# Four chained layers on one core: how the second layer divides by its denominators and projects, with a new planner table

## The chip, the cores and the metric

The kernel runs on one core of one Trainium2 chip. The metric is device time in microseconds (us). Before the change the median of three runs is 1347.23 us (1346.31 to 1350.47). The engines are PE (matrix multiply, writes to the accumulation banks `ps`), ACT (activation functions), DVE (vector work), POOL (a second, slower elementwise engine) and SP, whose queue issues the DMAs.

## The reference

```python
x = A_x                                   # 2048 rows, 512 columns, bfloat16
x = x + A(layernorm(x)); x = x + B(layernorm(x))
x = x + A(layernorm(x)); x = x + B(layernorm(x))

def A(x):   # attention, 32 heads of 16, one k and one v for all heads
    q = x @ wq;  k = x @ wk;  v = x @ wv
    return softmax(q @ k.T / 4) @ v  (heads side by side) @ wo
def B(x):   # linear attention, 32 heads of 16
    q, k, v = x @ wqkv
    pq, pk = phi(q), phi(k)               # phi(t) = (t + 1 if t > 0 else exp(t)) + 1e-6
    kv = sum over rows of pk (outer) v    # per head 16 x 16
    z  = sum over rows of pk              # per head 16
    return (pq @ kv) / (pq @ z + 1e-6) @ wo
```

Layers 0 and 2 are A, layers 1 and 3 are B.

## The kernel before, in words

Rows are handled in 16 tiles of 128. `x_sb` holds all of x, `XT` the transposed normalised tiles, `QT` the transposed queries (in layers 1 and 3 phi of the queries), all in SBUF.

**Layers A.** A layer has 2048 blocks of scores, each 128 keys by 512 (four heads by 128 queries); the two layers together have 4096. PE makes a block (line 1185, "QK"), then its exponential is taken in one of two ways. ACT takes two or three blocks in one instruction (line 1376, `128x1024` or `128x1536`). DVE takes one block with an approximate integer exponential (line 1480, called the fast exponential below), after which POOL makes three shifted copies of it, four blocks at a time (line 1522, `INT64_ADD`). PE multiplies the results with the values and adds them up (line 1239). DVE and POOL may take blocks only once the keys of tiles 0 to 7 exist in that layer; the code's name is `KGATE` = 7, called the gate below. The keys `KM` of tiles 4 to 7 are one group, written by line 1051 (ACT) or 1052 (DVE). On PE, line 1286 is filler without use for the result.

**Layers B.** Each tile gets phi of k, q and v: the exponential on ACT (line 1659), then two steps on DVE (lines 1661 or 776, and 1666). Sums over the rows are gathered in groups of four tiles (`KVG`) and end with the last tile, which is the last tile that layer A gives, so all of a layer B's outputs wait for the end of layer A.

In layer 1 the values lie in `va` with a column of ones behind every 16, so that one product gives kv and z together (line 1923). At the end DVE masks them to block-diagonal form (`kvz`, `zb`, lines 1945, 1949). Then, tile by tile: `den` multiplies `QT` with `zb` (lines 1971, 1973), DVE takes the reciprocal (line 1977); `main` multiplies `QT` with `kvz` (lines 1998, 2029), DVE multiplies with the reciprocals (2002, 2033, into `OB`), the result is transposed (on PE for tiles 0 to 3, by DMA, "va<-va", for tiles 4 to 15, into `OTB`), multiplied with `wo2` and added to x (for tiles 0 and 1 in halves, lines 910, 923, 942; else line 2061).

Layer 3 is built otherwise (`kvt`, `mix`, `den3`, `main3`): kv is multiplied with `wo2` once, giving four matrices M, and a tile's queries are divided by the denominators before one product with M ends the layer.

**Order.** A planner inside the program plays the kernel through with a duration for each operation and writes down the order of each engine's instructions. On the chip every engine runs its list in that order, and an instruction waits where its inputs aren't there. Durations, priorities and the table `TABLE` (from which planned time which set of the planner's numbers holds) so decide how many blocks go to ACT and how many to DVE. The layer-2 tiles follow layer 1 as its outputs come; `MW` and `DW` hold a tile of layer 1 back until a given tile of layer 2 has its normalised rows.

Of the kernel before, what the change touches and what calls it, by code (L numbers as in the profile page):

```python
# [420 lines left out]
class Seg:  # L421
# [46 lines left out]
NOB = 4  # L468
# [29 lines left out]
DENS = {1: [[0], [1], [2], [3], [4], [5], [6], [7], [8, 9], [10, 11], [12, 13], [14, 15]]}  # L498
# [52 lines left out]
MCOP = (DV,)*4  # L551
EVP = 1.2
# [20 lines left out]
    (840, dict(AHEAD=10, BLT=2.2, EVP=1.2, HMAX=0.35, HTOL=0.02, STICK=1.0)),
    (930, dict(AHEAD=10, BLS=1.9, BLT=2.2, EVP=1.2, HMAX=0.35, HTOL=0.02, STICK=1.0)),
    (1110, dict(HMAX=0.1, SPX=1.5, STICK=0.5)),
    (1290, dict(BLS=2.3, BLX=1.0, EVP=0.95, HMAX=0.1, SPX=3.0, STICK=0.5)),
]
BASE = dict(AHEAD=AHEAD, BLS=BLS, BLT=BLT, BLX=BLX, CHT=CHT, DPP=DPP, DXB=DXB, EVP=EVP, FBS=FBS, HMAX=HMAX, HTOL=HTOL, LOW=LOW, OWNP=OWNP, SPX=SPX, STICK=STICK)


def bass_interleave_layers__grouped_kv_mqa__linear_attn_block__prompt_kernel(
# [46 lines left out]
    ones1 = sb("ones1", [1, P], BF16)  # L628
# [1503 lines left out]
```

## Time and profile before

| | |
|---|---|
| runs | 1347.23 us median (1346.31, 1347.23, 1350.47) |
| profiled execution | 1346.96 us, of which 1345.2 us span from first to last instruction, 1.8 us around it |
| granted PE clock | 1.000 |
| ACT busy | 1314.6 us (98%) |
| PE busy | 1301.1 us (97%), with filler |
| DVE busy | 1225.8 us (91%) |
| POOL busy | 1077.2 us (80%) |

A group's row in the profile gives a line, the engine, the shape, a count, the busy time of the group and the mean duration of one. Where instructions overlap at their ends, busy time divided by the count is less than the mean duration: it is what one more of them costs an engine that is full. "Idle before" is the time for which the engine stood still ahead of the group. A timeline row gives start and length in us.

### The profile page before, as it was taken

To read this page: it belongs to the slowest core of one execution; us is meant where nothing else is said; L and a number is where in the kernel's file an instruction comes from. 1 tells how busy PE (TensorE), PEld (TensorE's weight loads), DVE (VectorE), ACT (ScalarE), POOL (GpSimd) and SP (SyncE) were. 2 spreads that over 40 slices of the span, in tenths; PEclk is the share of its full clock that TensorE was granted. 3 is DMA by queue.
4 is the path that set the end of the run, shared out by engine and by line. 5 is a ranking of instruction groups with operands and counts; after the bars stand their busy time and mean duration, and the time that the engine had idled before them with its cause. 6 is when DMAs were issued, how large, how long until landed. Compare 5 with 4: busy or idle time off the path is not lost.

```text
span 1345.2 us, 39031 instructions
## 1 busy us (share of the span) xinstructions
PE 1301.1 (97%) x15334; PEld 436.1 (32%) x15391; DVE 1225.8 (91%) x2224; ACT 1314.6 (98%) x1523; POOL 1077.2 (80%) x1085
## 2 busy tenths in 40 slices
PE   9999999999999999999999999999999999999998
PEld 4322323322232222223643323332232323232335
DVE  8899999899899999997889899989999899999977
ACT  8999999999999999999799999999999999999996
POOL 1699898899989999997005797879989798989870
PEclk9999999999999999999999999999999999999999
DMA  4300000000000000000022000000000000000001
GB/s 107 99 6 13 6 6 13 6 13 2 14 6 13 7 6 6 2 1 2 2 44 45 9 6 13 18 6 6 13 7 9 6 13 6 6 6 1 2 2 64
DMA packets 52517, 20.64 MB, mean 15 GB/s; under 512 B 46192, under 2 KB 51824, under 8 KB 52336
## 3 DMA queue, kind: packets, MB, share of 16 engines
q1 hardware_dynamic: 51280, 18.10, 6.0%
q8 instruction: 125, 2.05, 0.6%
q14 instruction: 56, 0.46, 0.1%
q10 hardware_dynamic: 1056, 0.03, 0.0%
HBM read 5.28 MB, written 2.10 MB: 5 GB/s over the span
## 4 chain that ended last, share of the span: by engine, by line
PE 49%; ACT 30%; issue 9%; DVE 8%; POOL 2%; DMA 1%; ACTq 0%; POOLq 0%; DVEq 0%
ACT W L1376 29%; PE ps L1239 20%; PE ps L1185 16%; PE ps L861 5%; DVE W L1480 4%; PE ps L1064 3%; POOL W L1522 2%; PE ps L904 2%; PE ps L1286 1%; ACT phE L1659 1%; PE ps L1170 1%; DVE sacc L1540 1%; DVE sacc L1666 0%; DVE xn L776 0%; DMA W<-xn 0%
## 5 line engine op out<-in xcount | busy, mean ns | idle before, releaser
L1376 ACT ACTIVATE W<-ps 128x1024 bf16<-128x1024 f32 (+1 forms) x1322 | 1257.4, 1157 | 1.7 <-PE ps L1185 1.5
L1522 POOL INT64_ADD W<-W x1047 | 1070.1, 1036 | 228.2 <-DVE W L1480 174.0
L1480 DVE TENSOR_SCALAR W<-ps 128x512 int16<-128x512 f32 x1394 | 902.8, 682 | 65.9 <-PE ps L1185 54.7
L1239 PE MATMUL ps<-W,VV 128*32 128x512 bf16 x8278 | 631.3, 384 | 3.6 <-DVE sacc L1540 2.4
L1185 PE MATMUL ps<-W,KM 32*128 32x512 bf16 x4096 | 517.6, 385 | 22.2 <-ACT W L1376 12.9
L1185 PEld LDWEIGHTS ps<-W,KM 32*128 32x128 bf16 x4096 | 129.9, 91 | 513.0 <-ACT W L1376 448.0
L1239 PEld LDWEIGHTS ps<-W,VV 128*32 128x32 bf16 x8278 | 149.2, 94 | 250.7 <-issue 176.2
L861 PE MATMUL ps<-wqkv,W 128*128 128x512 bf16 (+1 forms) x226 | 66.8, 368 | 8.0 <-issue 5.1
L1286 PE MATMUL ps<-W,V 128*32 128x512 bf16 (+5 forms) x229 | 61.1, 336 | 1.2 <-DVE W L1666 0.3
L1659 ACT ACTIVATE phE<-ps 128x512 bf16<-128x512 f32 (+1 forms) x66 | 44.4, 675 | 5.2 <-PE ps L1064 4.0
L1540 DVE STREAM_TRANSPOSE sacc<-ps 128x512 f32<-128x512 f32 x52 | 36.8, 707 | 10.1 <-PE ps L1239 10.1
L964 DVE BATCH_NORM_STATS2 st<-x_sb 128x6 f32<-128x512 bf16 x60 | 40.6, 680 | 1.2 <-DMA x_sb<-in_A_x_dram 0.9
L904 PE MATMUL ps<-wo,OT 128*32 128x512 bf16 (+1 forms) x544 | 40.5, 372 | 0.4 <-DVE W L855 0.4
L1064 PE MATMUL ps<-W,wqkv 128*128 128x128 bf16 x512 | 39.5, 220 | 0.4 <-DVE W L855 0.4
L1064 PE MATMUL ps<-W,wq 128*128 128x128 bf16 x464 | 35.6, 220 | 0.6 <-DVE W L1480 0.5
L1064 PEld LDWEIGHTS ps<-W,wqkv 128*128 128x128 bf16 x512 | 29.9, 98 | 10.3 <-issue 7.8
L1064 PEld LDWEIGHTS ps<-W,wq 128*128 128x128 bf16 x464 | 26.1, 98 | 13.7 <-issue 10.4
L776 DVE TENSOR_SCALAR phE<-phE 128x513 bf16<-128x513 bf16 x50 | 21.1, 422 | 10.1 <-ACT phE L1659 8.9
L776 DVE TENSOR_SCALAR xn<-x_sb,mv,rs 128x513 bf16<-128x513 bf16 x52 | 27.0, 532 | 1.8 <-ACT rs L955 1.7
L861 PEld LDWEIGHTS ps<-wqkv,W 128*128 128x128 bf16 x272 | 17.6, 97 | 30.9 <-issue 20.1
L1579 DVE TENSOR_TENSOR Osb<-sacc,ps 128x256 bf16<-128x256 f32 x64 | 26.0, 407 | 0.4
L1286 PEld LDWEIGHTS ps<-W,V 128*32 128x32 bf16 x229 | 18.2, 95 | 24.5 <-issue 10.6
(145 smaller groups left out, 514.3 us busy)
## 6 DMA issues: line engine op xcount, KB each, us to landing
out_dram<-x_sb SPq DMA_DIRECT2D x16, 128.0 KB, 1.7
x_sb<-in_A_x_dram SPq DMA_DIRECT2D x6, 256.0 KB, 5.2
wqkv<-in_B_wqkv_dram SPq DMA_DIRECT2D x1, 1536.0 KB, 8.4
W<-xn SPq DMA_TRANSPOSE x46, 2.5
x_sb<-in_A_x_dram SPq DMA_DIRECT2D x4, 128.0 KB, 2.2
wq<-in_A_wq_dram SPq DMA_DIRECT2D x1, 512.0 KB, 4.3
wo<-in_A_wo_dram SPq DMA_DIRECT2D x4, 128.0 KB, 3.1
wo<-in_B_wo_dram SPq DMA_DIRECT2D x1, 512.0 KB, 9.3
```

Source lines behind the costliest of these rows:

```text
L776: return e.add_instruction(mybir.InstTensorScalarPtr(name=nc.get_next_instruction_name(), engine=mybir.EngineType.DVE, op0=op0, op1=op1, i ...
L861: return e.matmul(dst, lhsT=l, rhs=r, start=(k == 0), stop=(k == len(pairs) - 1))
L904: ins = e.matmul(ps[32 * q:32 * q + 32, b * 512 + cs.start:b * 512 + cs.stop], lhsT=l[:, q, :], rhs=r, start=start, stop=stop)
L1064: ins = e.matmul(dst[:, g * P:(g + 1) * P], lhsT=lhs(g, k), rhs=rhs(k), start=(k == 0), stop=(k == FT - 1))
L1185: return e.matmul(bank(b), lhsT=KM[r, sg.par, kt * P:(kt + 1) * P], rhs=QT[r, sg.t, :], start=True, stop=True)
L1239: ins = e.matmul(ps[32 * j:32 * j + 32, ACC * 512:(ACC + 1) * 512], lhsT=VV[:, kt, 0 if w is None else 1 + w, :], rhs=ap, start=(k == 0), ...
L1286: o = op({PE: (n / 2400.0, lambda e: e.matmul(ps[32 * j:32 * j + 32, b * 512:b * 512 + n], lhsT=V0[:], rhs=QT[:, sg.t, 0:n], start=st, sto ...
L1376: ex = op({AC: (EXO + 0.4267 * n, lambda e, n=n, s_=s_, p_=p_: e.activation(ws_(p_), ps[:, s_ * 512:(s_ + n) * 512], ACTF.Exp, scale=EXPSC ...
L1480: o = op({DV: (0.602, lambda e: e.tensor_scalar(out=dst.bitcast(I16), in0=bank(b), scalar1=VB, scalar2=VLO, op0=ALU.add, op1=ALU.max))}, w ...
L1522: o = op({PO: (512 * m * PSR + PSO, lambda e, g_=g_, f_=f_: e.int64_add(ws_(g_).bitcast(I64), ws_(f_).bitcast(I64), step))}, reads=wk_(f_) ...
L1540: o = op({DV: (TRD, lambda e, src=src: e.transpose(src, bank(ACC)))}, writes=[B_(ACC)] + key, prio=0.0, lat=0.15)
L1659: op({AC: (0.07 + n / 1200.0, lambda e: e.activation(phE[:, i, 0:n], bank(b, n), ACTF.Exp))}, reads=[B_(b)], writes=[("phE", i)], prio=pr ...
```

## The change

In layer 1 the old `kv_`, `den` and `main` go, and the way of layer 3 is used with another way to divide:

- `kvt` now serves layer 1 too: values without the column of ones between heads (the sums z are a product with one column of ones), and M = kv times `wo2` by `mix`, whose four copies from the banks go DVE, ACT, DVE, ACT (`MCO1`). M lies in `va` 0 to 3, kv in `va` 5.
- `denc` makes the denominators of four tiles at once, compact: 16 matmuls with `ZC` (32 columns each) put head h of tile j on row 32j + h of one bank, 128 columns of queries. One Ln and one Exp with scale -1 on ACT (128x128 each) give the reciprocals, in `va` 4.
- `norm1` spreads each reciprocal over the head's 16 rows and multiplies `QT` with it: for tiles 0 to 3 by four matmuls with a constant `E4` (made on POOL at the start) and a DVE multiply from the bank; for tiles 4 to 15 by four DMAs on SP's queue from 8 rows to 128 rows, 256 bytes each, into one of three buffers, and a DVE multiply of two SBUF operands. After the gate of layer 2 that multiply runs over a rearranged order of elements (`turn`).
- `main3` multiplies the divided queries with M and adds x (tiles 0 and 1 in halves).
- Gone per tile: the reciprocal on DVE, the product with `kvz`, the DVE multiply of its 512 columns from a bank, the transpose and its copy.
- The value product of layers 0 and 2 (`a_v`) has 16 columns instead of 128.
- The late tiles' queries of layer 1 have a pool of their own (`NB1`), and `TABLE` is another one.

```diff
@@ a_v
-            mm(v[:, i, :], [(XT[:, t, ft, :], wkv[:, ft, 0:P]) for ft in range(FT)], [XK_(t), "wv", "wkr"], b, prio, 0.25)
+            mm(v[:, i, 0:DH], [(XT[:, t, ft, :], wv[:, ft, :]) for ft in range(FT)], [XK_(t), "wv"], b, prio, VDUR)
@@ table
-    (840, dict(AHEAD=10, BLT=2.2, EVP=1.2, HMAX=0.35, HTOL=0.02, STICK=1.0)),
...
+    (840, dict(AHEAD=10, BLS=1.9, BLT=2.9, BLX=1.0, DXB=0.3, HMAX=0.2, HTOL=0.06, LOW=6, OWNP=4.0, SPX=4.0)),
...
@@ kvt, at the end, L == 1
+                    o = op({DV: (0.13, lambda e, b=bs[1]: e.tensor_tensor(
+                        out=ZC[:].rearrange("p (g c) -> p g c", c=40)[:, :, 0:8], in0=bank(b, 4).unsqueeze(2).to_broadcast([P, 4, 8]),
+                        in1=mask8[:, :, 0:1].rearrange("p h o -> p (h o)").unsqueeze(1).to_broadcast([P, 4, 8]), op=ALU.mult))},
+                           reads=["mask8"], writes=[B_(bs[1]), "ZC"], prio=pr - 0.05)
+                    pl.process(denc(0, DENC[0], bs[1]))
@@ mix
-            c = op({MCOP[g]: by[MCOP[g]]} if MCOP else by, writes=[B_(b), ("W", g), ("M", g)], prio=pr)
+            c = op({MCOP[g]: by[MCOP[g]]} if L == 3 else {MCO1[g]: by[MCO1[g]]}, writes=[B_(b), MK(g), ("M", g)], prio=pr, over=under(g))
@@ new: denc and norm1
+            def fn(e):
+                for g in range(4):
+                    for j, t in enumerate(ts):
+                        ins = e.matmul(ps[32 * j:32 * j + 32, b * 512:b * 512 + P], lhsT=ZC[:, 32 * g:32 * g + 32], rhs=QT[:, t, g * P:(g + 1) * P],
+                                       start=(g == 0), stop=(g == 3))
+            op({PE: (0.3, fn)}, reads=[QK_(t) for t in ts] + ["ZC"], writes=[B_(b)], prio=pr, lat=0.2, mode="col").cols = 512
+            op({AC: (DC1[0], lambda e: e.activation(bank(b, P), bank(b, P), ACTF.Ln, bias=epsc[:]))}, reads=["epsc"], writes=[B_(b)], prio=pr if pl.calm else 0.9)
+            o = op({AC: (DC1[1], lambda e: e.activation(vm_(4)[:, P * gi:P * gi + P], bank(b, P), ACTF.Exp, scale=-1.0))}, writes=[B_(b), ("rec", gi)],
+                   prio=pr - 0.01 if pl.calm else 0.9, over=[("va", 4)])
...
+            if t not in PEX:
+                i = yield ("acq", rb_pool, pr)
+                rb = vm_(i)
+                for g in range(4):
+                    op({SP: (0.07, lambda e, g=g: e.dma_start(rb[:, g * P:(g + 1) * P], vm_(4)[32 * j + 8 * g:32 * j + 8 * g + 8, P * gi:P * gi + P].unsqueeze(1).to_broadcast([8, DH, P])))},
+                       reads=[("rec", gi)], writes=[("rb", i, g)], prio=pr, lat=DBL, dma=True, over=[("va", i), "kvT"] if i == 5 else [("va", i)])
+                yield from until(*[("rb", i, g) for g in range(4)])
+                if ("K", 2, KGATE) in pl.flags:
+                    o = op({DV: (0.6, lambda e: e.tensor_tensor(out=turn(q), in0=turn(q), in1=turn(rb), op=ALU.mult))},
...
+                else:
+                    o = op({DV: (0.34, lambda e: e.tensor_tensor(out=q, in0=q, in1=rb, op=ALU.mult))},
...
+            op({PE: (0.23, fn)}, reads=[("rec", gi), ("E4", j)], writes=[B_(b)], prio=pr, lat=0.2).cols = 512
+            o = op({DV: (0.6, lambda e: e.tensor_tensor(out=q, in0=q, in1=bank(b), op=ALU.mult))}, writes=[B_(b), QK_(t), ("qn", t)], prio=pr)
@@ main3, now for layer 1 too
+            if t in MCRIT[L]:
+                bs = yield from acq2(pr)
+                proj2(bs, lambda g: qn[:, g * P:(g + 1) * P], lambda g, hs: at(g)[:, hs], t, keys, pr)
...
-        def kv_(gi, ts):
-        def den(ts):
-        def main(t):
...
```

Line numbers move by up to 13 before layer B's code: the exponentials are lines 1376 and 1480 before and 1387 and 1491 now, QK is 1185 and 1196, layer 1's addition to x is 2061 and 1986. Counted over the whole order of the engines, these counts differ:

| engine, operation | before | now |
|---|---|---|
| ACT exponential, two blocks (`128x1024`) | 1264 | 1259 |
| ACT exponential, three blocks (`128x1536`) | 58 | 58 |
| ACT exponential, one block (`128x512`) | 0 | 1 |
| DVE fast exponential, one block | 1394 | 1403 |
| of these in layer 0 / layer 2 | 718 / 676 | 715 / 688 |
| ACT Ln and Exp of `denc` (`128x128`) | 0 | 8 |
| ACT copy of M (`128x512`) | 0 | 2 |
| ACT copy of `OTB` (`128x512`, `128x256`) | 1, 2 | 0, 0 |
| ACT `KM` (`128x512`, `128x256`) | 3, 2 | 2, 0 |
| DVE `KM` (`128x512`, `128x256`) | 9, 2 | 10, 4 |
| SP transposes of `va` / spreading DMAs | 12 / 0 | 0 / 48 |

**ACT between layer 1's last sums and layer 2's first normalisation.** Before (phE is phi's exponential, x_sb the addition to x, va the copy of a transposed tile, ve and rs the normalisation):

```order
L1696 CAST va<-ps 128x16x16 x2
L1659 ACTIVATE phE<-ps 128x512 x2
L877 COPY va<-ps 128x256
L942 CAST x_sb<-ps 128x256
L877 COPY va<-ps 128x256
L942 CAST x_sb<-ps 128x256
L953 ACTIVATE ve<-mv,eps 128x1
L955 ACTIVATE rs<-ve 128x1
```

Now:

```order
L1707 CAST va<-ps 128x256 x2
L1672 ACTIVATE phE<-ps 128x512
L1911 ACTIVATE ps<-ps,epsc 128x128
L1912 ACTIVATE va<-ps 128x128
L1852 CAST va<-ps 128x512
L1672 ACTIVATE phE<-ps 128x512
L1852 CAST va<-ps 128x512
L1672 ACTIVATE phE<-ps 128x512
L953 CAST x_sb<-ps 128x256 x2
L964 ACTIVATE ve<-mv,eps 128x1
L966 ACTIVATE rs<-ve 128x1
```

Ln and Exp (1911, 1912) and two of the four copies of M (1852) stand now between the last sums and the addition to x; the copies of transposed tiles are gone.

**DVE in the same place.** Before (zb and kvz are the masks, rdB the reciprocals, L2002 the multiply with them, L936 the statistics of x):

```order
L1945 TENSOR_TENSOR zb<-ps,mask 128x8
L1945 TENSOR_TENSOR zb<-ps,mask 128x24
L1949 TENSOR_TENSOR kvz<-ps,mask 128x128
L1949 TENSOR_TENSOR kvz<-ps,mask 128x384
L1977 RECIPROCAL rdB<-ps 128x32 x2
L1661 TENSOR_SCALAR phE<-phE 128x512
L2002 TENSOR_TENSOR va<-ps,rdB 128x256 x4
L876 COPY va<-ps 128x256
L1666 SCALAR_TENSOR_TENSOR W<-ps,phE 128x512
L1661 TENSOR_SCALAR phE<-phE 128x512
L936 BN_STATS st<-ps 128x6 x2
```

Now (ZC and the mask of kv, the copies of M, the multiply of the queries in `W`):

```order
L1817 TENSOR_TENSOR ZC<-ps,mask 128x4x8
L1829 TENSOR_TENSOR va<-ps,mask 128x512
L1674 TENSOR_SCALAR phE<-phE 128x512
L1852 CAST va<-ps 128x512
L1959 TENSOR_TENSOR W<-W,ps 128x512
L1852 CAST va<-ps 128x512
L1959 TENSOR_TENSOR W<-W,ps 128x512
L1679 SCALAR_TENSOR_TENSOR W<-ps,phE 128x512
L947 BN_STATS st<-ps 128x6 x2
```

Two copies of M and two multiplies stand now where the reciprocals, four half multiplies and a copy stood.

**PE where the keys of tiles 4 to 7 are made in layer 2.** W,wkv with 512 columns is their product (four matmuls), W,KM is QK, wkv,W the value product, W,VV the product with the values. Before:

```order
L1185 MATMUL ps<-W,KM 128x512 x3
L861 MATMUL ps<-wkv,W 128x128 x3
L861 MATMUL ps<-W,wkv 128x512
L1185 MATMUL ps<-W,KM 128x512 x2
L861 MATMUL ps<-W,wkv 128x512 x3
L861 MATMUL ps<-wkv,W 128x128 x4
```

Now:

```order
L872 MATMUL ps<-wkv,W 128x16 x8
L1250 MATMUL ps<-W,VV 32x512 x4
L1196 MATMUL ps<-W,KM 128x512 x3
L872 MATMUL ps<-W,wkv 128x512 x3
L1196 MATMUL ps<-W,KM 128x512 x2
L872 MATMUL ps<-W,wkv 128x512
```

The rows look alike, but the place is another: counted from layer 2's first QK, the last matmul of these keys stands behind 84 blocks of QK before and behind 64 now.

More of the change, by code (lines that the diff above doesn't have):

```diff
@@ L467 @@
 RING = 24
-NOB = 4
 DTL = 3.6
@@ L551 @@
 MCOP = (DV,)*4
+MCO1 = (DV, AC, DV, AC)
+DC1 = (0.31, 0.26)
+SPL = False
+DCP = 1.3
+NB1 = 3
+VDUR = 0.16
+PEX = range(4)
+DBL = 2.6
 EVP = 1.2
@@ L1872, in main3 @@
         def main3(t):
             pr = 1.5 + 0.02 * t
-            yield ("flag", ("qn", t))
+            yield ("flag", ("qn", L, t))
             for g in range(4):
-                yield ("flag", ("M", g))
+                yield ("flag", ("M", L, g))
             yield from until(("qn", t), *[("M", g) for g in range(4)])
+            if L == 1 and MW[t] is not None:
+                yield ("flag", ("xnT", 2, MW[t]))
+                yield from until(XK_(MW[t]))
+            qn = QT[:, t, :] if L == 1 else W[:, 4 + t, :]
@@ L2067, in main @@
+            if L == 1 and t in QHOLD[2]:
                 lend_after(("x", L, t), NW + t)
@@ L2071, in run_b @@
             pl.process(q_(t))
-            pl.process((main3 if L == 3 else main)(t))
-        for ts in DENS.get(L, ()):
-            pl.process(den(ts))
+            pl.process(main3(t))
         if L == 3:
```

328 lines of the change are left out of this document (110 added, 218 removed).

## The prediction

> **What bounds the kernel now.** I read the page's first part, then the busy time of every engine by stretches.
>
> ```profile
> span 1345.2 us, 39031 instructions
> PE 1301.1 (97%) x15334; PEld 436.1 (32%) x15391; DVE 1225.8 (91%) x2224; ACT 1314.6 (98%) x1523; POOL 1077.2 (80%) x1085
> ```
>
> ```profile
> core 0: us, PE busy (x) PEld busy (x) DVE busy (x) ACT busy (x) POOL busy (x), PEclk, DMA share, GB/s
> 0.00:50.00 50.00, 45.66 (x439) 21.96 (x440) 41.50 (x107) 43.62 (x59) 11.91 (x43) 1.00 0.53 136
> 50.00:600.00 550.00, 538.20 (x6432) 160.20 (x6449) 516.46 (x894) 549.76 (x617) 515.58 (x507) 1.00 0.04 8
> 600.00:660.00 60.00, 57.92 (x771) 31.00 (x769) 48.94 (x114) 50.10 (x78) 29.59 (x31) 1.00 0.01 2
> 660.00:700.00 40.00, 38.09 (x378) 17.83 (x382) 29.98 (x62) 39.52 (x49) 0.00 (x0) 1.00 0.20 36
> 700.00:1300.00 600.00, 580.43 (x6903) 182.25 (x6927) 557.54 (x981) 599.29 (x682) 512.26 (x500) 1.00 0.05 10
> 1300.00:1345.20 45.20, 40.84 (x427) 22.85 (x431) 31.39 (x69) 32.29 (x43) 7.81 (x8) 1.00 0.14 48
> ```
>
> PE and ACT both look full, but PE's time holds filler, and ACT is the one without gaps: from 50 to 600 us it stands still for 0.24 us, from 700 to 1300 for 0.71. Its 30.6 us of idle time (1345.2 - 1314.6) lie at the start (6.4 in the first 50 us), at the passage from layer 0 through layer 1 to layer 2 (9.9 between 600 and 660) and at the end (12.9). So the time is ACT's work plus the idle time of these three places, and a change counts by what it does to either. DVE and POOL matter because each block that DVE takes is one that ACT needn't, and these blocks begin only at the gate. POOL's 0.00 between 660 and 700 shows where layer 2 runs without that help.
>
> What an exponential costs ACT, and the other ACT rows that the change touches:
>
> ```profile
> L1376 ACT ACTIVATE W<-ps 128x1024 bf16<-128x1024 f32 x1264 | 1183.9, 1140 | 1.4 <-PE ps L1185 1.3
> L1376 ACT ACTIVATE W<-ps 128x1536 bf16<-128x1536 f32 x58 | 85.5, 1521 | 0.3 <-PE ps L1185 0.2
> L1051 ACT ACTIVATE KM<-ps,kmask 128x512 bf16<-128x512 f32 x3 | 2.1, 712 | 1.4 <-DVE KM L1052 1.4
> L1051 ACT ACTIVATE KM<-ps,kmask 128x128 bf16<-128x128 f32 x5 | 1.8, 364 | 0.6 <-PE ps L861 0.5
> L1727 ACT CAST va<-ps 128x512 bf16<-128x512 f32 x2 | 1.4, 704 | 0.0
> L1051 ACT ACTIVATE KM<-ps,kmask 128x256 bf16<-128x256 f32 x2 | 0.9, 473 | 0.3 <-PE ps L861 0.2
> L877 ACT COPY va<-ps 128x256 bf16<-128x256 bf16 x2 | 0.7, 373 | 0.0
> L855 ACT COPY va<-ps 128x512 bf16<-128x512 bf16 x1 | 0.6, 580 | 0.0
> ```
>
> Two blocks cost 1183.9 / 1264 = 0.937 us, three 85.5 / 58 = 1.474, so a third block costs 0.54 and one alone about 0.5 (0.937 less a block of the first kind, half of it).
>
> **The change part by part.** *ACT's exponentials.* By the counts, five instructions of two blocks go and one of one block comes: -5 x 0.937 + 0.5 = **-4.2 us**. The nine blocks go to DVE. Where from: layer 2 gives DVE 12 more, layer 0 three fewer. The layer-2 gain is the earlier gate: the keys of tiles 4 to 7 stand behind 64 QK blocks instead of 84, and 20 blocks at half of 0.937 are 9.4 us of ACT. In the trace the gate is here:
>
> ```profile
> 700.20 0.75 DVE L1052 TENSOR_SCALAR KM<-ps,kmask 128x512 bf16<-128x512 f32 x1 [1.75 <-PE ps L861]
> 700.86 0.68 DVE L1480 TENSOR_SCALAR W<-ps 128x512 int16<-128x512 f32 x1
> ```
>
> *ACT's other work.* The eight Ln and Exp of 128x128 are in no row; the same shape as `KM` takes 0.364, so 8 x 0.36 = +2.9 (bounds 1.5, half of it, where their ends overlap, to 3.8, with the 0.473 of the row of 256 columns). Two copies of M at 0.704: +1.4. Three copies of transposed tiles: -0.58 - 2 x 0.37 = -1.3. `KM` on ACT: -0.71 - 2 x 0.47 = -1.65. Together **+1.35**. [...]
>
> *A wait that goes.* At 44 us ACT stood still behind DVE for the second half of a group of layer 0's keys; in the new order ACT writes both halves of one itself there:
>
> ```profile
> 44.15 0.69 ACT L1051 ACTIVATE KM<-ps,kmask 128x512 bf16<-128x512 f32 x1 [1.35 <-DVE KM L1052]
> ```
>
> That is **-1.35** of ACT's idle time. What is late next there is PE's matmul for these keys, which both halves wait for in either order; if it comes late too, half of it returns.
>
> *The passage.* The chain from the last sums to layer 2's first exponential, and the gaps in it:
>
> ```profile
> 644.17 0.41 PE L1923 MATMUL ps<-va,sacc 128*128 128x136 bf16 x4
> 644.64 0.25 DVE L1945 TENSOR_TENSOR zb<-ps,mask 128x8 bf16<-128x8 f32 x2
> 645.50 0.56 DVE L1977 RECIPROCAL rdB<-ps 128x32 f32<-128x32 f32 x2
> 646.24 1.42 DVE L2002 TENSOR_TENSOR va<-ps,rdB 128x256 bf16<-128x256 f32 x4
> 647.93 0.78 PEld L923 LDWEIGHTS ps<-wo,va 128*128 128x128 bf16 x8
> 648.60 0.87 DVE L936 BATCH_NORM_STATS2 st<-ps 128x6 f32<-128x256 f32 x2
> 655.84 1.06 PE L1089 MATMUL ps<-W,wq 128*128 128x128 bf16 x16
> 657.36 0.39 PE L1185 MATMUL ps<-W,KM 32*128 32x512 bf16 x2
> 657.79 1.02 ACT L1376 ACTIVATE W<-ps 128x1024 bf16<-128x1024 f32 x1 [0.48 <-PE ps L1185]
> ```
>
> Before, the sums end at 644.58 and the projection of tile 0 starts 3.4 us later. Now there are two strands. Denominators: mask 0.25, 16 matmuls about 0.5, Ln 0.36, Exp 0.36, four spreading matmuls 0.4, with about 0.3 for the handing over, ready for the multiply at 2.3. M: mask of kv, matmul, four copies, two of them on DVE. DVE must do mask 0.6, copy 0.6, multiply 0.6, copy 0.6 in that order, with waits for the first matmul and for the spreading: the fourth ends at about 3.6. So tile 0 comes some 0.2 us later than before; tile 1, whose multiply follows at once, some 0.4 earlier than its transposes and copies let it. Behind that, the first QK stood behind the 16 matmuls of tile 1's queries (655.84, 1.06 us); in the new order it stands ahead of them, waiting only for tile 1's keys. DVE's order has two more long steps (0.6 each) before tile 0's statistics, which takes most of that back. I take **-0.5**, with bounds of -1.5 (all of the 1.06 and tile 1's 0.4) and +1.5 (two DVE steps of 0.6 with waits). ACT's additional work in the passage is counted above.
>
> *The spreading DMAs.* A transposing issue holds SP for 1.19 us, a plain one less:
>
> ```profile
> L2086 SPq DMA_DIRECT2D out_dram<-x_sb x16: 332/332/368, 1327.2 to 1342.9; - x16
> out_dram<-x_sb SPq DMA_DIRECT2D x16, 128.0 KB, 1.7
> L869 SPq DMA_TRANSPOSE va<-va x12: 1188/1190/2096, 672.9 to 731.8; - x12
> va<-va SPq DMA_TRANSPOSE x12, 2.8
> ```
>
> At 0.33 us an issue and 1.7 to landing, four DMAs of a tile land 3 x 0.33 + 1.7 = 2.7 us after they may start, about what one transpose took. Three buffers let the first three tiles go at once: the third lands after 11 x 0.33 + 1.7 = 5.3 us, and the planner reckons 0.07 an issue and 2.6 to landing, 3.4 in all. DVE's list has the third multiply right behind the first two, so it waits up to 2 us there, and behind it are queued phi's steps, whose banks PE wants. DVE has 10.0 of 40 us free between 660 and 700, and ACT then has tile 0's and 1's blocks to go on with: I take **+0.5**, bounds 0 to +2. The 48 issues take 16 us of SP in place of 12 x 1.19 = 14.3; the transposes of layer 2's rows queue behind them, which is in the same half us.
>
> *What counts nothing.* PE loses work in both the value product and layer 1; ACT doesn't wait for it in the long stretches (1.3 us before 1264 exponentials, first row above), so it becomes filler. The constants on POOL come before its first blocks, in 38 us of the first 50 that are free; if they came late, only tiles 0 to 3 of layer 1 would ask for them, 600 us later.
>
> Sum against the profiled execution: 1346.96 - 4.2 + 1.35 - 1.35 - 0.5 + 0.5 = **1342.8 us**. That execution lies 0.27 below the median of the runs, so against the median of 1347.23 the forecast is 0.33% faster. What a measurement of this kernel can tell from no change is about 0.3%, 4 us: below 1343.2 counts as faster, above 1351.3 as slower. The forecast lies only 0.4 inside.
>
> **The rivals.** *1. DVE and POOL collide, no change to speak of.* The multiply of the spread reciprocals has two SBUF operands. Before, such a multiply ran only at the end, with POOL still:
>
> ```profile
> L1867 DVE TENSOR_TENSOR W<-W 128x512 bf16<-128x512 bf16 x16 | 6.1, 418 | 0.0
> L1522 POOL INT64_ADD W<-W x1047 | 1070.1, 1036 | 228.2 <-DVE W L1480 174.0
> ```
>
> In the new order four or five of them come behind the gate, with POOL at work. If the two engines exclude each other, each may wait one POOL addition: 4 x 1.04 = 4.1 us on a DVE that is 93% full from there on (557.54 of 600), passed on through PE to ACT: 1346.9, the same as before. [...] No run here shows it, and four tiles have little weight; I give it 0.15.
>
> *2. The gain is eaten by small waits, no change.* The work saved on ACT is only 2.85 us; if the passage goes to its upper bound and the DMAs too, the sum is 1346.96 - 4.2 + 1.35 - 1.35 + 1.5 + 2 = 1346.3. For it speaks that two unlike orders meet the chip's durations with other slack; against it that ACT stood still for under 1 us in 1150 us of the long stretches. This, and smaller misses of the kind that leave the time between 1343.2 and 1346, have 0.22.
>
> *3. The DMAs are slow, slower than before.* If a spreading DMA holds SP as a transpose does, 1.19 us, and lands after 2.8, the third tile lands after 11 x 1.19 + 2.8 = 15.9 us instead of 5.3. DVE, PE and ACT run in order, so most of the 10.6 comes through, less what DVE's slack takes: about 10 us, 1352.8. It turns slower from 8.5 us on, that is from about 1.05 us an issue. A plain issue of 0.33 speaks against it; the broadcast of one row to 16 and the 256 bytes are in no row. 0.11.
>
> *4. The change does less than the order says:* the keys of tiles 4 to 7 are late on the chip and DVE's additional blocks hold up PE. That is rival 2 with the place at the gate; it has no chance of its own.
>
> **How the numbers follow.** The forecast has 0.52, rivals 1 and 2 (no change) 0.37, rival 3 (slower) 0.11. The lower end takes the passage's and the activations' lower bounds: 1342.8 - 1.0 - 1.4 - 0.5 (no DMA wait) = 1339.9, and 1.5 more, since ACT's start and end may gain as the passage did: 1338.5. The upper end holds rivals 1 and 2 with half of a DMA term on top: 1346.9 + 1 = 1348. Rival 3 and a faster end beyond 1338.5 are left out, under 2 in 10.
>
> **What would show it.** Right: ACT's busy time near 1311.8 us; 1403 fast exponentials, the first of layer 2 some 8 us earlier in the span than 700.86; no gap ahead of `KM` at 44 us; ACT's idle time from 600 to 660 near 9.4; the four DMAs of a tile landing within 3 us. Wrong: ACT idle for more than 2 us between 660 and 1300 (rivals 2 and 3, told apart by whom DVE's multiply of the queries waits for), a multiply of 1 us or more beside POOL (rival 1), or an issue of a spreading DMA near 1 us.

## The result and the profile after

The changed kernel takes **1359.72 us** (median of 4 runs, 1357.32 to 1361.96) against 1348.49 for the kernel before (1346.31 to 1350.47; four runs, the three of the table above among them). The ratio is 1.0083, interval 1.0062 to 1.0105: slower by 0.83%. The forecast was 1342.8, faster. The profiled execution took 1360.89 us.

The page of the changed kernel, span and engines:

```profile
span 1359.1 us, 39265 instructions
PE 1321.0 (97%) x15441; PEld 434.8 (32%) x15441; DVE 1237.8 (91%) x2219; ACT 1315.0 (97%) x1523; POOL 1089.3 (80%) x1094
```

Busy time by stretches of the changed kernel, cut as in the prediction (last columns: granted TensorE clock, DMA share, GB/s):

```profile
0.00:50.00 50.00, 45.79 (x430) 20.47 (x430) 39.78 (x105) 42.95 (x59) 12.65 (x45) 0.93 0.53 138
50.00:600.00 550.00, 542.09 (x6478) 161.90 (x6476) 513.63 (x887) 549.92 (x616) 511.49 (x502) 1.00 0.04 7
600.00:660.00 60.00, 59.80 (x797) 30.13 (x794) 49.79 (x105) 51.58 (x80) 33.05 (x33) 1.00 0.01 2
660.00:700.00 40.00, 36.29 (x361) 16.92 (x360) 32.25 (x73) 34.82 (x51) 0.00 (x0) 0.96 0.30 43
700.00:1300.00 600.00, 581.70 (x6781) 178.28 (x6780) 557.62 (x962) 589.16 (x662) 512.71 (x498) 0.98 0.05 9
1300.00:1359.10 59.10, 55.37 (x604) 27.08 (x604) 44.69 (x93) 46.52 (x60) 19.44 (x19) 1.00 0.11 37
```

ACT's work hardly changed (1315.0 against 1314.6). Its idle time rose from 30.6 to 44.1 us, and the rows say where: 5.18 us between 660 and 700 where it was 0.48 (+4.7), and 10.84 between 700 and 1300 where it was 0.71 (+10.1); the start loses 0.7, the passage and the end win 1.8. The clock column has numbers below 1.00 in the rows of 660 and 700, and at the start. A finer cut of the same view, first the kernel before, then the changed one:

```profile
660.00:680.00 20.00, 18.80 (x196) 9.20 (x197) 14.36 (x30) 19.60 (x24) 0.00 (x0) 1.00 0.09 15
700.00:720.00 20.00, 18.93 (x183) 6.28 (x184) 19.43 (x37) 19.74 (x25) 9.34 (x9) 1.00 0.13 27
720.00:740.00 20.00, 18.20 (x166) 5.83 (x168) 18.59 (x34) 19.84 (x27) 10.55 (x11) 1.00 0.26 52
740.00:760.00 20.00, 19.12 (x218) 6.42 (x216) 16.90 (x31) 19.97 (x25) 14.31 (x14) 1.00 0.07 15
```

```profile
660.00:680.00 20.00, 16.60 (x178) 8.99 (x177) 14.26 (x32) 14.94 (x22) 0.00 (x0) 0.91 0.32 41
700.00:720.00 20.00, 15.76 (x101) 3.83 (x103) 19.21 (x28) 14.79 (x17) 6.72 (x5) 0.78 0.27 42
720.00:740.00 20.00, 18.23 (x166) 5.14 (x158) 18.42 (x31) 16.71 (x19) 12.06 (x11) 0.84 0.12 21
740.00:760.00 20.00, 19.99 (x195) 5.37 (x195) 17.67 (x31) 18.03 (x22) 15.06 (x15) 0.87 0.07 15
```

So nearly the whole loss lies in two places: ACT works 4.7 us less between 660 and 680 and 10.0 less between 700 and 760. The timeline of the second, in DVE's, PE's, POOL's and ACT's rows (start, length, and in brackets the idle time ahead with what ended it):

```profile
704.47 2.45 DVE L1941 TENSOR_TENSOR W<-W,va 128x512 bf16<-128x512 bf16 x1
...
706.98 0.39 PE L872 MATMUL ps<-va,W 128*128 128x512 bf16 x1 [1.41 <-DVE W L1941]
...
707.54 4.87 POOL L1533 INT64_ADD W<-W  x3 [71.32 <-DVE W L1491]
...
707.96 2.91 DVE L1941 TENSOR_TENSOR W<-W,va 128x512 bf16<-128x512 bf16 x1
...
711.45 0.61 PE L1196 MATMUL ps<-W,KM 32*128 32x512 bf16 x3 [2.24 <-DVE W L1491]
...
712.10 1.02 ACT L1387 ACTIVATE W<-ps 128x1024 bf16<-128x1024 f32 x1 [2.42 <-PE ps L1196]
```

`L1941` is the multiplication of the queries behind the gate, the one whose operands go through `turn`: its view `p (g c) -> p c g` with 128 columns in `c` makes neighbouring elements lie 128 columns apart. It takes 2.45 us, and did so the first time with POOL still idle; the same multiplication ahead of the gate (`L1944`, no `turn`) takes 0.42. Four of them hold DVE for 8 us more than the plan's 0.6 each, PE stands still behind them, and then PE itself is slow: three QK matmuls take 0.61 us at 711.45, at a granted clock of 0.50, where they took 0.39 at 703.35, at 1.00.

The first place, 660 to 680, in the same view, with the rows for the spreading DMAs' line (duration min/median/max) and DVE's wait for them (total, times, longest) ahead:

```profile
L1937 SPq DMA_DIRECT2D va<-va x48: 607/607/807, 658.4 to 709.3; - x48
```

```profile
DVE W L1944 <- DMA va<-va: 4.2, 2, 2.2
```

```profile
665.61 0.42 DVE L1944 TENSOR_TENSOR W<-W,va 128x512 bf16<-128x512 bf16 x1 [2.25 <-DMA va<-va]
...
666.43 1.70 PE L872 MATMUL ps<-va,W 128*128 128x512 bf16 x4 [2.16 <-DVE W L887]
668.35 0.42 DVE L1944 TENSOR_TENSOR W<-W,va 128x512 bf16<-128x512 bf16 x1 [1.98 <-DMA va<-va]
...
669.01 0.60 ACT L1672 ACTIVATE phE<-ps 128x512 bf16<-128x512 f32 x1 [3.31 <-PE ps L1075]
```

An issue holds SP for 0.607 us, not 0.33. The second and third multiplication wait for their DMAs; PE, in order, stands still for 2.16 us, runs four matmuls in 1.70 us behind that, and ACT waits 3.31. The clock fell here too: 0.91 on the average of these 20 us.

### The profile page after: what moved, and what is told of

Read it like the earlier page. It is cut to its first block, busy times and chain, and to the rows that moved or that the text cites. A ratio compares the mean times of both kernels' runs of the same rounds, so it can differ in the third digit from the quotient of the medians.

```text
span 1359.1 us, 39265 instructions
## 1 busy us (share of the span) xinstructions
PE 1321.0 (97%) x15441; PEld 434.8 (32%) x15441; DVE 1237.8 (91%) x2219; ACT 1315.0 (97%) x1523; POOL 1089.3 (80%) x1094
## 4 chain that ended last, share of the span: by engine, by line
PE 52%; ACT 29%; issue 8%; DVE 8%; POOL 3%; DMA 1%; SPq 0%; ACTq 0%; DVEq 0%; POOLq 0%
ACT W L1387 27%; PE ps L1250 22%; PE ps L1196 17%; PE ps L872 4%; PE ps L1075 3%; POOL W L1533 3%; DVE W L1491 2%; PE ps L1297 2%; PE ps L915 2%; ACT phE L1672 1%; DVE st L975 1%; DVE xn L781 0%; DVE W L1941 0%; SPq L1937 0%; DVE KM L1063 0%
## 5 line engine op out<-in xcount | busy, mean ns | idle before, releaser
L1491 DVE TENSOR_SCALAR W<-ps 128x512 int16<-128x512 f32 x1403 | 912.0, 682 | 71.1 <-PE ps L1196 58.1
L1250 PE MATMUL ps<-W,VV 128*32 128x512 bf16 x8305 | 638.5, 386 | 4.6 <-DVE sacc L1551 3.1
L1250 PEld LDWEIGHTS ps<-W,VV 128*32 128x32 bf16 x8305 | 152.0, 94 | 260.4 <-issue 169.8
L872 PE MATMUL ps<-wqkv,W 128*128 128x512 bf16 (+1 forms) x272 | 76.5, 371 | 0.4 <-DVE sacc L1679 0.3
L1297 PE MATMUL ps<-W,V 128*32 128x512 bf16 (+6 forms) x243 | 67.8, 352 | 1.7 <-DVE W L866 0.8
L1075 PEld LDWEIGHTS ps<-W,wq 128*128 128x128 bf16 x464 | 26.2, 98 | 13.5 <-issue 9.5
```

The source lines that it names most:

```text
L872: return e.matmul(dst, lhsT=l, rhs=r, start=(k == 0), stop=(k == len(pairs) - 1))
L1075: ins = e.matmul(dst[:, g * P:(g + 1) * P], lhsT=lhs(g, k), rhs=rhs(k), start=(k == 0), stop=(k == FT - 1))
L1250: ins = e.matmul(ps[32 * j:32 * j + 32, ACC * 512:(ACC + 1) * 512], lhsT=VV[:, kt, 0 if w is None else 1 + w, :], rhs=ap, start=(k == 0), ...
L1297: o = op({PE: (n / 2400.0, lambda e: e.matmul(ps[32 * j:32 * j + 32, b * 512:b * 512 + n], lhsT=V0[:], rhs=QT[:, sg.t, 0:n], start=st, sto ...
L1491: o = op({DV: (0.602, lambda e: e.tensor_scalar(out=dst.bitcast(I16), in0=bank(b), scalar1=VB, scalar2=VLO, op0=ALU.add, op1=ALU.max))}, w ...
```

## The experiments

Three theories stood after the result: **A**, the turned order of elements makes the multiplication slow by itself (rival **B**: it collides with POOL); **C**, the DMAs' issues, one behind another, set the wait at 660 (rival **D**: the landing does); and **E**, the new order or its table is to blame for all of it.

**1. Plain multiplications.**

```
-    e.tensor_tensor(out=turn(q), in0=turn(q), in1=turn(rb), op=ALU.mult)
+    e.tensor_tensor(out=q, in0=q, in1=rb, op=ALU.mult)
```

> Edit: the four multiplications of the queries behind the gate read and write their columns in plain order instead of the turned one (stride of 128 columns inside); every instruction stands where it stood in the changed kernel. Theory A (shape): the turned multiplication takes 2.43 us by itself, whatever POOL does; it holds DVE, PE stands still behind it and its granted clock halves. Then the plain ones take 0.42 us with POOL at work, the clock stays at 1.00 between 700 and 760 us, ACT's busy time there returns from 49.5 to about 59.5 us, and the time is 1359.7 - 10 = about 1349.5 us. Rival B (collision): the multiplication is long because POOL is at work. Then the plain ones take 1 to 1.5 us (0.42 and up to one POOL addition of 1.04), the clock still falls once or twice, and the time is 1354 to 1359 us.

Measured: 1349.05 us (10 runs, 1345.8 to 1351.39), ratio to before 1.0001 (0.9988 to 1.0015). By stretches, and the rows of the four multiplications, with those of POOL's additions during which two of them ran:

```profile
660.00:680.00 20.00, 16.53 (x165) 7.99 (x162) 13.85 (x32) 15.36 (x22) 0.00 (x0) 0.91 0.27 35
700.00:720.00 20.00, 18.94 (x178) 5.67 (x176) 20.00 (x40) 20.00 (x24) 9.39 (x9) 1.00 0.32 50
720.00:740.00 20.00, 19.81 (x215) 5.97 (x215) 19.50 (x37) 20.00 (x24) 16.31 (x16) 1.00 0.11 21
740.00:760.00 20.00, 19.35 (x219) 6.09 (x215) 18.53 (x31) 20.00 (x22) 17.92 (x18) 1.00 0.01 2
```

```profile
702.25 0.42 DVE L1941 TENSOR_TENSOR W<-W,va 128x512 bf16<-128x512 bf16 x1
703.87 0.90 DVE L1941 TENSOR_TENSOR W<-W,va 128x512 bf16<-128x512 bf16 x1
707.98 0.40 DVE L1941 TENSOR_TENSOR W<-W,va 128x512 bf16<-128x512 bf16 x1
722.18 0.39 DVE L1941 TENSOR_TENSOR W<-W,va 128x512 bf16<-128x512 bf16 x1
...
703.45 3.35 POOL L1533 INT64_ADD W<-W  x3 [69.78 <-PE ps L1297]
...
721.22 3.38 POOL L1533 INT64_ADD W<-W  x3 [2.93 <-PE ps L1250]
```

A is shown, with every row in its old place. ACT works 60.00 of the 60 us from 700 to 760 (49.53 in the changed kernel) at the full clock. Of the two multiplications that ran beside POOL's additions, one took 0.90, 0.5 longer, and one 0.39. The trace of experiment 7, with the same order, has 0.90 at the same place and 0.42 and 0.40 for its other two plain ones. So a lengthening like the one B speaks of is seen at that one place, and costs DVE 0.5 us in the whole kernel. In the changed kernel POOL loses more than DVE: a group of three additions beside a turned multiplication takes 4.87 us (row of 707.54) where it takes 3.35 here. The loss between 660 and 680 is untouched.

**2. The planner is told the price of an issue** (turned multiplications kept, order planned anew).

```
-    op({SP: (0.07, lambda e, g=g: e.dma_start(rb[...], ...))}, ..., lat=DBL, ...)   # DBL = 2.6
+    op({SP: (0.61, lambda e, g=g: e.dma_start(rb[...], ...))}, ..., lat=DBL, ...)   # DBL = 2.4
```

> Edit: the planner is told that a spreading DMA holds SP for 0.61 us and lands 2.4 us after that, in place of 0.07 and 2.6; the order is planned anew, the turned multiplications stay. Theory C (issue): the loss between 660 and 680 us comes from the issues, one behind another on SP, for which the plan had left no time. Then DVE's wait for the DMAs (4.2 us) goes to under 0.5, ACT's busy time from 660 to 680 rises from 14.9 to 19 or more, and the time is about 1359.7 - 4.7 = 1355 us, with the loss behind 700 us still there. Rival D (the landing, or the passage itself): the wait stays above 2 us or is replaced by another on PE before 680 us, and the time stays at 1358 or above.

Measured: 1359.22 us, ratio 1.0079 (1.0055 to 1.0103).

```profile
660.00:680.00 20.00, 19.47 (x216) 10.32 (x215) 18.14 (x42) 19.34 (x30) 0.00 (x0) 1.00 0.35 47
...
700.00:720.00 20.00, 15.48 (x125) 4.36 (x122) 19.07 (x29) 14.15 (x17) 7.03 (x8) 0.84 0.17 26
720.00:740.00 20.00, 19.86 (x144) 4.30 (x142) 15.45 (x27) 15.37 (x17) 9.12 (x10) 0.66 0.08 15
```

DVE's wait for the DMAs is gone, and ACT works 19.34 of the 20 us from 660 on at the full clock, as C said. The time did not follow: the new order has 1394 fast exponentials in place of 1403, so the exponentials cost ACT 1271.5 us in place of 1266.5. In all ACT has 3.1 us more work (1318.1 against 1315.0), which takes back the 3.3 us of idle time that went (40.8 against 44.1). The four turned multiplications (2.54 us on the average) cost what they did before: ACT works 49.51 of the 60 us from 700 on. The wait is settled, C's time was missed by 4 us.

**3. and 4. Spreading by matmuls**, for all tiles, and for tiles 4 to 7 beside plain multiplications:

```
-PEX = range(4)
+PEX = range(16)        # 3: all tiles
+PEX = range(8)         # 4: with plain multiplications
```

> Edit: the reciprocals of all 16 tiles are spread by matmuls into PSUM, as those of tiles 0 to 3 are already; there are no spreading DMAs and no turned multiplication. Theories A and C together: both losses go, 10 us behind 700 and 4.7 between 660 and 680, while twelve multiplications read PSUM at 0.64 us in place of 0.42 (+2.6 us on DVE, not on ACT): about 1359.7 - 14.7 = 1345 us, at most 1348. Rival E (the new order or its table is to blame): the granted clock falls again in the same places, and the time stays above 1352 us.

Measured: 1348.93 us (10 runs), ratio 1.0009 (0.9993 to 1.0025). ACT is busy for 19.28 us from 660 to 680 and for all 60 from 700 to 760, at a clock of 1.00. Both losses are gone with the new table still in place, so the table isn't their cause; the order was planned anew, and for the order it is experiment 1 that speaks. That it isn't below 1348, as expected, has two reasons: the replanned order leaves ACT 1317.5 us of work in place of the 1312.5 with plain multiplications, and 5 of the 10 runs have a mean clock of 0.998 or less (median of the others 1347.5).

> Edit: plain multiplications, and the reciprocals of tiles 4 to 7 are spread by matmuls too, so that DMAs spread only tiles 8 to 15, which are wanted later. Theories A and C: no wait of DVE for DMAs over 0.5 us, the granted clock at 1.00 from 660 to 760 us, and the time 1344 to 1347 us. If the multiplications of tiles 8 to 15 collide with POOL (B), they take 1 us or more each, and the time is 1348 or above. Rival E as for the kernel without DMAs: above 1352 us.

Measured: 1357.81 us, ratio 1.0071 (1.0046 to 1.0096). A miss: this order leaves ACT 1320.6 us, DVE waits for DMAs for 4.9 us at other places ahead of the gate (3.21 of them at 680.30), and the start lost 2 us against before at a clock of 0.87. A small edit changes everything behind it in the plan; so of the experiments below all but the last keep the rows of PE, DVE and ACT where they were, apart from two DMA issues on ACT in experiment 6.

**5. Two queues for the early DMAs.**

```
-    op({SP: (0.07, lambda e, g=g: e.dma_start(rb[...], ...))}, ...)
+    op({PO if t < 8 and g > 1 else SP: (0.07, lambda e, g=g: e.dma_start(rb[...], ...))}, ...)
```

> Edit: plain multiplications, and of the four spreading DMAs of each of tiles 4 to 7 two go out on POOL's queue, where POOL stands still until the gate; PE, DVE and ACT keep the order of the changed kernel row for row. Theory C (the issues, one behind another on SP, set the wait): DVE's 4.4 us of waiting for the DMAs go to under 1, ACT's busy time from 660 to 680 rises from 15.4 to 19 or more, and the time falls by 3.5 to 4.5 us against the kernel with plain multiplications (1349.05 as median, 1345.8 in its runs at the full granted clock): to about 1342 at the full clock, 1345 as a median. Rival D (the landing sets it, or POOL's queue is as slow): the wait stays above 2.5 us and the time does not move by 2.

Measured: **1344.53 us** (12 runs, 1342.34 to 1348.84), ratio to before **0.9974** (0.9962 to 0.9986): faster than both kernels. The line's rows, DVE's wait, and the stretch:

```profile
L1939 SPq DMA_DIRECT2D va<-va x40: 607/607/850, 655.8 to 705.8; - x40
L1939 POOL DMA_DIRECT2D va<-va x8: 590/621/787, 656.1 to 661.6; - x8
...
DMA to landing us min/median/max: 2.5/2.8/4.5
```

```profile
DVE W L1946 <- DMA va<-va: 2.2, 1, 2.2
```

```profile
660.00:680.00 20.00, 17.36 (x176) 8.62 (x176) 15.12 (x34) 16.48 (x24) 1.18 (x2) 0.91 0.21 29
```

Half of the wait went, from 4.4 to 2.2, and the median fell by 4.5 us against plain multiplications. Only 2.2 of these lie in the runs at the full clock (1343.6 against 1345.8, table of experiments 8 to 10); the rest comes with fewer runs at a low clock, 5 of 12 in place of 7 of 10. C expected a wait under 1 us and holds for half of it; the other half is left to the landing (D) or to the issues that remain. Two of each early tile's four issues, at 0.607 us each, are gone from SP's row of issues.

**6. Three queues.**

```
+    op({AC if t < 6 and g == 3 else PO if t < 8 and g in (1, 2) else SP: (0.07, ...)}, ...)
```

> Edit: plain multiplications, and the spreading DMAs of the early tiles go out on three queues (tiles 4 and 5: one on SP, two on POOL, one on ACT; tiles 6 and 7: two on SP, two on POOL), PE, DVE and ACT otherwise in unchanged order. Theory C (the number of issues ahead of a tile's last DMA sets the wait): the wait of 2.2 us for tile 5 that is left with two queues falls under 1.2, the two issues on ACT cost it at most 1 us in a gap, and the time is 0.5 to 1.5 us under that of the kernel with POOL's queue alone (1342.3 to 1344.3 in its runs at the full clock). Rival D (the DMA engines, which work at 0.2 to 0.35 of their time, or the landing set it): the wait stays at 2 us or more, and the time is the same or, by the issues on ACT, up to 1 us longer.

Measured: 1346.09 us (12 runs, 1343.21 to 1349.43), ratio 0.9981 (0.9969 to 0.9994). The wait was 1.4 in place of 2.2, not under 1.2 as C expected, and ACT works 18.49 us from 660 to 680 in place of 16.48, at a clock of 1.00 in place of 0.91; from 600 to 660 it loses 0.6. In the runs at the full clock the time is 1343.3 against 1343.6, but 8 of 12 runs, not 5, had a lower clock, the profiled one among them, which lost 1.0 us between 20 and 40 at a clock of 0.91. The third queue's gain is thus at most 0.3 us, and the median is not below that of two queues. Nor is the shorter wait shown to be its work: the kernel of experiment 9, with two queues, waits 1.5 us in its trace (0.40 and 1.09), at a clock of 1.00 and with 18.29 us of ACT.

**7. One turned multiplication**, tile 15's, the other three plain.

> Edit: of the four multiplications behind the gate only that of tile 15 is turned; the other three are plain, every instruction stands where it stood. It tells the stall from what follows it. Theory K (the clock): the turned multiplication takes 2.43 us in place of 0.4; PE stands still behind it for over 1 us, and its granted clock then lies at 0.50 for 8 to 10 us, in which PE does 4 to 5 us less; ACT loses 3 to 4.5 us in all, most of them after the multiplication has ended: 1348.8 to 1350.3 at an otherwise full clock, against 1345.8. Rival L (the stall alone): ACT loses at most the 2.0 us by which the multiplication is longer, all of it within 3 us of its end, and the clock stays at 1.00: 1347.8 at most.

Measured: 1352.02 us (12 runs, 1348.27 to 1356.99), 3.0 above the kernel with four plain ones. It starts at 725.34 and takes 2.45 us; by stretches of 2 us:

```profile
726.00:728.00 2.00, 0.19 (x3) 0.11 (x2) 2.00 (x2) 1.53 (x2) 2.00 (x1) 1.00 0.33 66
728.00:730.00 2.00, 1.94 (x13) 0.51 (x12) 1.86 (x4) 0.97 (x2) 1.42 (x3) 0.80 0.00 0
730.00:732.00 2.00, 2.00 (x17) 0.57 (x13) 1.86 (x4) 1.99 (x3) 1.90 (x2) 0.50 0.00 0
732.00:734.00 2.00, 2.00 (x18) 0.47 (x20) 1.27 (x4) 1.04 (x3) 1.04 (x1) 0.50 0.00 0
734.00:736.00 2.00, 2.00 (x19) 0.30 (x14) 1.27 (x3) 1.51 (x2) 0.00 (x0) 0.50 0.00 0
736.00:738.00 2.00, 2.00 (x23) 0.56 (x22) 1.81 (x4) 2.00 (x5) 1.61 (x2) 0.99 0.00 0
```

PE stands still for 1.88 us, starts again at the full clock, and 1.2 us later is granted half of it for 6.8 us. In the rows above ACT loses 3.0 us: 1.50 up to 730, in the stall and just behind it, and 1.46 while PE feeds it at half speed. So K holds for the fall of the clock and the size of the loss, though half of that is the stall's, and L, which kept the clock at 1.00, is refuted. Two of the 12 runs have a mean clock of 0.999 and still take 1348.3 and 1348.4, 2.5 above the plain kernel's 1345.8. The plain kernel's trace has that mean clock with 3.4 us at half speed, so 6.8 us more don't fit; the clock fell for less time in these two runs, but where is not known.

The trace of the changed kernel says more of this. Its stretches at a granted clock of 0.50 begin at 35.19, 666.65, 711.03 and 734.92 and last 6.83, 3.41, 10.24 and 10.24 us, near one, two and three times 3.41; the last three begin 44.38 and 23.89 us apart, near 13 and 7 times 3.41. Why is not shown. The three after 600 us begin in or behind gaps of PE of 2.16, 2.24 and 1.66 us (1.88 in this experiment); behind its gaps of 1.41 us (at 705.57), 0.97, 0.85 and 0.77 the clock stayed at 1.00 for at least 3.4 us, as it did behind the longest gaps between matmuls in the kernel before, 0.63 to 0.88. At the start this doesn't hold: in the 3.41 us ahead of 35.19 PE stood still for 0.62 us, in two gaps of 0.32 and 0.30.

**8. to 10. The value product and the start.** In the changed kernel the clock also fell between 35 and 42 us (0.88 from 20 to 40), with no gap of PE over 0.4 us just ahead. Three kernels asked whether the thin value product does that: plain multiplications with 128 columns again; the same with POOL's queue; the kernel before with 16.

```
-    mm(v[:, i, 0:DH], [(XT[:, t, ft, :], wv[:, ft, :]) for ft in range(FT)], ...)          # 16 columns
+    mm(v[:, i, :], [(XT[:, t, ft, :], wkv[:, ft, 0:P]) for ft in range(FT)], ...)           # 128 columns
```

> Edit: plain multiplications, and the value product writes 128 columns again as before the change (112 of them unused), in unchanged order. Theory F: the thin product leaves PE emptier in the first 40 us, and so the granted clock halves there for some 5 us in most executions (7 of 10 of the kernel with plain multiplications lie at a clock of 0.993 to 0.997, before 6 of 19); with 128 columns this happens in at most a third of the runs, and the median falls from 1349 to about 1346. Rival G (the waits of the start do it, not the product's width): more than half of the runs still lie under a clock of 0.998, and the median stays within 1 us of 1349.

> Edit: the two edits of the kernels with POOL's queue and with 128 columns together. If C and F both hold: no wait of DVE for DMAs above 1 us, a granted clock of 0.999 or more in two thirds of the runs, and a median of 1341 to 1343, below the kernel before by 0.3 to 0.45%. If one fails, about 1345; if both, 1349.

> Edit: the kernel before, with the value product at 16 columns instead of 128, and every instruction in its old place. Theory F (the thin product makes the granted clock halve in the first 60 us more often): where 13 of 48 runs of the kernel before lie at a clock of 0.998 or less, half or more do here, and the median rises by 1 to 3 us. Rival G (what makes it halve is the new order of the start): no more than a third do, and the median is the same as before or up to 1 us lower.

Measured, with the number of runs whose mean clock is 0.998 or less:

| kernel | median us | ratio to before (interval) | low clock | median of the others |
|---|---|---|---|---|
| before (three comparisons) | 1347.2 to 1347.4 | | 20 of 77 | 1347.0 |
| before, 16 columns | 1346.78 | 0.9994 (0.9981 to 1.0007) | 2 of 12 | 1346.8 |
| plain | 1349.05 | 1.0001 (0.9988 to 1.0015) | 7 of 10 | 1345.8 |
| plain, 128 columns | 1347.82 | 1.0007 (0.9999 to 1.0016) | 1 of 11 | 1347.8 |
| plain, POOL's queue | 1344.53 | 0.9974 (0.9962 to 0.9986) | 5 of 12 | 1343.6 |
| plain, POOL's queue, 128 columns | 1345.24 | 0.9991 (0.9980 to 1.0002) | 3 of 12 | 1345.2 |

In the new order the thin product goes with more of the low-clock runs (12 of 22 against 4 of 23), in the old order it does not (2 of 12 against 20 of 77): F as it was stated is refuted by the old order, G by the new one; it seems to take both the order and the width. A low clock goes with some 3 to 4 us more (1350.7 against 1347.0 in the kernel before). With 128 columns the other runs are 1.6 to 2.0 us longer, so that is what its steadiness costs. The kernel with both edits was expected at 1341 to 1343 if C and F held: its clock was as expected, but its waits of 1.5 us and its time were not. That these low clocks lie at the start is known only for the profiled executions.

**11. The old table** with plain multiplications.

> Edit: plain multiplications, and the planner's table of before in place of the new one; the order is planned anew. Its order has 1375 fast exponentials on DVE in place of 1403, and ACT 1223 of two blocks, 91 of three and 2 of one in place of 1259, 58 and 1: 1281 us in place of 1265.7. Theory H (the time follows ACT's work by these counts, and the table is a part of the change that can't be left out): about 15 us above the kernel with plain multiplications, 1360 to 1364. Rival E (the new table, its early gate above all, is what makes PE stand still): ACT's idle time between 660 and 760 goes, and the time is 1352 or below.

Measured: 1372.78 us, ratio 1.0189 (1.0169 to 1.0208).

```profile
L1385 ACT ACTIVATE W<-ps 128x1024 bf16<-128x1024 f32 x1223 | 1150.5, 1143 | 4.3 <-PE ps L1194 4.0
L1385 ACT ACTIVATE W<-ps 128x1536 bf16<-128x1536 f32 x91 | 134.3, 1561 | 12.5 <-PE ps L1194 12.4
```

The two forms cost ACT 1284.8 us where the plain kernel has 1265.8; that is H's 15 us and more, and 10.6 us of idle time come on top (42.6 against 32.0). Of the 42.6, 16.4 lie between 660 and 740, where DVE waits 15.1 us for the spreading DMAs. H's direction holds, the time is 9 us above its upper end, and E is out: with the old table the idle time of that place grew instead of going, and ACT's work with it.

## Why the prediction was wrong

Its base, that the time is ACT's work plus ACT's idle time at a few places, is the right ledger: 0.4 more work and 13.5 more idle time make the 13.9 of the span. The terms, against the changed kernel and against the kernel with plain multiplications, whose rows stand in the same order:

| term | predicted | changed kernel | plain multiplications |
|---|---|---|---|
| ACT's work in all | -2.85 | +0.4 | -2.1 |
| the wait at 44 us | -1.35 | none ahead of `KM`, but +0.7 in the first 50 us, at a low clock | -1.35 in the first 50 us |
| idle time from 600 to 660 | -0.5 | -1.5 | -0.7 |
| spreading DMAs (660 to 700) | +0.5 | +4.7 | +4.3 |
| idle time from 700 to 1300 | 0 | +10.1 | -0.3 |

**The step that failed first** is the price of the multiplications behind the gate. The prediction priced all twelve by rows of 0.418, in plain order, and let those behind the gate be lengthened only by POOL. That `turn` changes the order of the elements stood in the change and was costed at nothing (the diff's own plan had 0.6 for it against 0.34 for the plain form); no row of the kernel before has such an operand, so this was an operation without a row, and its bounds were not drawn. Four times 2.0 us or more on a DVE that is 93% busy, in front of a PE that runs in order, made 10.1 us, together with the third point below. Rival 1 named the right instruction, place and sign ("a multiply of 1 us or more") with another cause: the collision it stood on costs DVE 0.5 us in place of 4.1, and one multiplication beside POOL, of 0.39, shows none. The plain form that the kernel used ahead of the gate would have been the cheaper one behind it too.

**The second** is the term of the DMAs, mis-sized. The prediction took 0.33 us an issue and 1.7 to landing from the stores of the output; the issues take 0.607, and landing 2.5 to 4.5 (on POOL's queue, experiment 5). By its own formula the third tile comes after 11 x 0.607 + 2.8 = 9.5 us; in the trace DVE multiplies it at 668.35, 10.0 us after the first issue at 658.4. Rival 3 had this chain with 15.9 us. "Bounds 0 to +2" came from the same store's row, and the transpose's row, 1.19, was left to the rival; between two rows of unlike kind the range should have reached over both.

**The third** is what no term had: PE's clock. A stall was priced at its own length. In the traces PE, after standing still for 1.66 to 2.24 us in the changed kernel and 1.88 in experiment 7, worked at a granted clock of 0.50 for 3.4 to 10.2 us, and ACT, with 0.7 us of slack in 600, pays for that too. The second term holds some of it: from 660 to 680 ACT works 18.3 to 18.5 us in two traces without a fall and 16.5 in the one with two queues and a fall.

**What held.** The counts (1403 fast exponentials), the exponentials' price (1179.7 / 1259 = 0.937), Ln and Exp together (2.6 us measured against 2.9), the wait at 44 us and the passage. ACT's work came 0.7 higher than forecast with plain multiplications (1312.5), and 2.5 more in the changed kernel, 1.0 of it in the exponentials of two blocks, of which one behind a gap counts 1.02 us against the mean of 0.937; the rest was not traced. The first fast exponential of layer 2 came at 698.04, 2.8 us earlier and not 8; with plain multiplications, where the profiled run had no low clock at the start, it came at 695.82, with POOL's queue at 694.48. With both failed steps mended as far as the runs went, the change is worth 2.7 us, 0.26%. The forecast had 0.33%, which counts the 0.27 us by which its own starting point lay under the median; from 1346.96 to 1342.8 it is 0.31%.

What stays open: the 1.5 to 2.2 us that DVE still waits with two queues, whether a third queue shortens that, why the turned order costs DVE 2.45 us in place of 0.42, and what makes the clock fall at the start.

## What to carry to other kernels

When an edit gives an operation another access pattern, price it as an operation that the trace has never shown, however familiar its name and shape are, and look for a row with that pattern before anything else. Where the trace shows PE's granted clock fall behind a stall, count the stall at more than its length: here one of 1.88 us cost ACT 3.0 us, and one of 1.66 with 10.2 us at a clock of 0.50 behind it cost 4.2. Count a burst of small DMAs by the issue time of its own kind on its queue (0.607 us here), times the number ahead of the one that is waited for. In a static plan, separate a mechanism from its order: the experiment that moved no row gave a plain answer, while the three orders that were planned anew (experiments 2 to 4) had 8 to 13 fast exponentials fewer and 3 to 8 us more work for ACT, which hid the effect that was asked for.

## What the runs showed of the hardware

- A DVE multiplication of 128x512 bf16 took 0.39 to 0.43 us in plain order, POOL idle, and 2.43 and 2.45 with neighbouring elements 128 columns apart (changed kernel, 714.48 and 704.47), a factor of 5.8 whose cause the traces don't show. Beside POOL's additions the plain one took 0.39 and 0.90 (experiment 1), the turned one 2.46 and 2.91 (changed kernel) and 2.45 (experiment 7).
- A DMA between SBUF buffers that spreads 8 rows to 128 held SP's queue for 0.607 us (POOL's 0.62, ACT's two 0.62 and 1.24), where a store of 128 KB to memory took 0.33 and a transpose 1.19.
- PE's granted clock was 1.00 or 0.50 in nearly every slice of 2 us (changed kernel and experiment 7). Its stretches at 0.50 lasted 3.41, 6.83, 10.24 and 10.24 us in the changed kernel. After 600 us they began in or behind gaps of PE of 1.66 to 2.24 us (1.88 in experiment 7), and none within 3.4 us of its gaps of 0.77 to 1.41; at the start one began behind two gaps of 0.32 and 0.30 us, and with plain multiplications the clock was 1.00 from 0 to 60 us.
